# Two order strings rewritten, and one stride moved from a transpose's output to another's PSUM input, in an fp32 attention-and-SwiGLU kernel

## The chip, the cores and the metric

The kernel runs on one core of one Trainium2 chip. The metric is the device time of one execution in microseconds, as the median of several runs. The profile comes from one further execution.

## The reference

Eight batches of 512 tokens and 32 states, eight heads of 64. Tokens read the states and states read the tokens by softmax attention; the result of both, 544 rows of 512 per batch, goes through an RMS norm and a SwiGLU network of width 1536.

```python
scores = x @ state^T / 8;   a  = softmax(scores)    # per batch and head: 512 x 32
xread  = a @ state
scores2 = state @ x^T / 8;  a2 = softmax(scores2)   # 32 x 512
sread  = a2 @ x
rows = concat([xread, sread]) as (4352, 512)        # heads side by side
xn  = rows / sqrt(mean(rows^2) + 1e-6) * rms_g
out = (silu(xn @ w_gate) * (xn @ w_val)) @ w_out
```

Activations are fp32. The three weights come as 64-bit floats, which the kernel turns into fp32 itself from their bits.

## The kernel before, in words

The work is a set of Python generators, one for each kind of step. A `yield` ends a step, and strings of letters (`ORDER`, `PERIOD`, `STATES`) say in which order the steps are taken. The instructions of PE (TensorE), DVE (VectorE), ACT (ScalarE), POOL (GpSimd) and SP (the queue of most DMAs) stand in each engine's queue in just that order, so the strings are the schedule. Each engine works its queue in order and waits at the head of it.

**Batch 0 and the start (`ORDER`).** 18 weight pieces arrive as raw 64-bit words. Letter `e` is ScalarE's part of the conversion (L222, L224, L227), `d` VectorE's (L248, L251, L255, L260), four instructions of 128 by 1024 for a piece. Converted gate and value weights go out to a scratch tensor and are fetched again for each later batch. `a` and `A` are `tokens_read` of batches 0 and 1: load and transpose the tokens on TensorE (L306, copied by ScalarE at L308), scores (L333), transposes of scores (L342), softmax, and the read-out (L426), squares, and the norm: L353, POOL's power (L277), L284 along rows, and L439, which scales the attention weights. `s` and `S` are `states_read`. `v` multiplies a weight pair by the states (L554, copied at L566), so that `h`, `t`, `u` are hidden products with the attention weights (L597), their silu (L603) and gate (L607). `p` and `c` project (L803) and copy out. `k` sums output weights (L846). `z` is `keep_awake`, a matmul on the identity whose result nobody reads (L1135).

**Batches 1 to 7 (`PERIOD`).** The string is walked once per batch. Hidden products use seven products in place of eight (`hidden_seven`: L701 on TensorE, L747 to L754 on ScalarE, L763, L776 to L788 on VectorE), the projection seven times seven in place of 64 (`project_twice`: L1003; its inner sums are L1051 to L1057, its outer ones L1062, its additions L1043, its last combinations on POOL L1029 to L1034, stores at L1111). While batch b is multiplied, the tokens and states of batch b+1 are read (`a`, `s`). For batches 2 to 7, the transposes of the tokens don't run on TensorE: VectorE transposes 32 by 32 blocks (L316), a DMA writes them to scratch (L318, on ScalarE's queue) and four read them back across partitions (L323). Each token tensor is loaded so that four consecutive tokens lie in one partition, which leaves the columns of the scores in an order that has to be put right somewhere. Letters `q` and `G` (sums of weight quarters, and the first fetches of them) have steps in batch 1 alone; a letter with no stream is skipped.

In the last period no batch follows. There the letter `a` takes steps of `state_norm` (L519, L524, L528, the power, L284, then L534 and L686 in one step) and of the sums of the first weight piece for the states (L658 to L664), but through `paced`, which lets eleven calls pass and then takes one step in three calls.

**The states (`STATES`).** At last all 256 state rows go through the network by L701 and L866.

Of the kernel before, what the change touches and what calls it, by code (L numbers as in the profile page):

```python
# [8 lines left out]
F32 = mybir.dt.float32  # L9
# [4 lines left out]
ACTF = mybir.ActivationFunctionType  # L14
# [3 lines left out]
P = 128  # L18
# [1 line left out]
W_BUFS = 3  # L20

ORDER = (
    "aaaaaadaaaaadeeaaeaaeadaaaeeaaaeaaadaadeaaeadddzzzzzzzzzzzzzzzzzzzzzzzzaaadaddee"
    "daaaeazzzzzzzzzzzvvzaddeadvazzzAeeadeaedzzzhtdddAehAuAhdAeAeeAAtdpdddedpddvvvhue"
    "hddeeAehddteeppdudhdededApdvpddsdtshusevevhAeedehtApdAdeAAeupeedhdAdtApddhAvAsev"
    "uvsdApdhAetdsdhphAepeAsedAtesddeesuddpAddshdudApevdvpsAvAsheeedAdthheudAedtpeAdd"
    "dAApeddAApehuvvvApedhSShtAhAdduSdhASStSpASSAASukkkSpAkwSSsswwSwpwckcSkkpkkkpckck"
    "wwww"
)

PERIOD = (
    "vfhththahhtalhhuxxuttqqhufxtvqhhhtahahuuqquuutqhaquhaqttahhhhxthhuxquutxhuhuttuv"
    "kkqxxxvxhaqqhhGthhqqauuuxxqqqhkaatuGhqkuuthuaattaaahuqaqhuhuthtsusushhhuutthhGug"
    "huuqqpqtpaauufhuagpkuppkkpqsaakfgkkappcpkpakkcqkpkppapppppcqqkkkkpakppppppkppkpp"
    "pcaaaaaksssaaqaaakpppckkpppksappkskkagggcksakaakppppaooaoposkppppgkkkpasakoawssw"
    "xosspxfxlccoowxxxf"
)
# [8 lines left out]
def kernel(  # L46
# [32 lines left out]
    SCALE = 1.0 / D ** 0.5  # L79
# [3 lines left out]
    one = ctx.enter_context(tc.tile_pool(name="one", bufs=1))  # L83
# [206 lines left out]
    def scores(b, packed, soft):  # L290

        xb = x_sb[b]
        stT = one.tile([P, 4, Ns], F32, name="stT")
        tp = aps.tile([P, 4, Ns], F32, name="at")
        TE.transpose(out=tp.rearrange("p j n -> p (j n)"),
                     in_=packed.rearrange("p e d -> p (e d)"), identity=ident)
        yield
        VE.tensor_copy(stT, tp)
        yield "step"

        if b < 2:
            xT = one.tile([P, 4, NC, P], F32, name="xT", tag="xT")
            for c in range(NC):
                tp = aps.tile([P, 4, P], F32, name="at")
                for j in range(4):
                    TE.transpose(out=tp[:, j, :], in_=xb[:, c, P * j:P * j + P], identity=ident)  # L306
                yield
                SE.copy(xT[:, :, c, :], tp)  # L308
                yield "step"
            xT = xT.rearrange("p j c t -> p j (c t)")  # L310
        else:


            xB = one.tile([P, 4, 4, Ns, NC], F32, name="xB", tag="xT")
            for q in range(4):
                VE.transpose(out=xB[:, q].rearrange("p j t c -> p j c t"), in_=xb[:, q // 2::2, :, Ns * (q % 2):Ns * (q % 2) + Ns])  # L316
                yield
            nc.scalar.dma_start(out=x_d[b % 2].rearrange("q g f r -> (g f) q r"),  # L318
                                in_=xB.rearrange("p q j t c -> p q (j t c)"))
            yield  # L320
            xT = one.tile([P, 4, 4, P], F32, name="xG", tag="xT")
            for q in range(4):
                nc.scalar.dma_start(  # L323
                    out=xT[Ns * q:Ns * q + Ns].rearrange("f g j r -> f g (j r)"),
                    in_=x_d[b % 2][q].rearrange("g f r -> f g r"))
                yield
            xT = xT.rearrange("p g j r -> p j g r")


        sp = [aps.tile([P, S], F32, name="at") for e in range(2)]  # L330
        for j in range(4):
            for e in range(2):
                TE.matmul(out=sp[e][Ns * j:Ns * j + Ns, :], lhsT=stT[D * e:D * e + D, j, :],  # L333
                          rhs=xT[D * e:D * e + D, j],
                          start=True, stop=True)
        yield


        sS = read[b] = (one if b else x_0).tile([P, 2, NC, P], F32, name="sS")
        eS = one.tile([P, 2, S // Ns, Ns], F32, name="eS", tag="eS")  # L340
        for e in range(2):
            VE.transpose(out=eS[:, e].rearrange("p k n -> p (k n)"), in_=sp[e])  # L342
# [100 lines left out]
    def states_read(b):  # L443

        xb, sS = x_sb.pop(b), read.pop(b)
        e2 = one.tile([P, 4, 2, NC, Ns], F32, name="e2")
# [8 lines left out]
        VE.tensor_scalar(s2, m2, -SCALE, None, op0=ALU.mult)  # L455
        yield
        for e in range(2):
            to = exps[:, e] if b < 2 else e2[:, :, e].rearrange("p g c t -> p g t c")
            SE.activation(out=to, in_=(sS[:, e] if b < 2 else
                                       sS[:, e].rearrange("p g (t c) -> p g t c", c=NC)), func=ACTF.Exp, scale=SCALE,  # L460
                          bias=s2[:, e:e + 1], accum_out=z2[:, e:e + 1])
            yield "step" if e else None

# [685 lines left out]
        for part in own:  # L1149
            yield from part[0]  # L1150

    def paced(steps):

        yield from range(11)
        while True:
            if next(steps, done) is done:
                break
            yield from range(3)
        while True:
            yield  # L1160

    parts_0, banks_0 = {}, []
    load_state(0)
    load_x(0, nc.scalar, nc.sync)
# [15 lines left out]
    with tc.manual_schedule(**by_hand):  # L1180
# [7 lines left out]
        for b in range(1, B):  # L1188
            h, t, u = hidden_seven(S, weights_of(b), lambda b=b: tokens_of(b), True)
            p, c, k, o = project_twice(b, store_tokens(b))  # L1190
            own = [own_weights(b, mp) for mp in range(2, NM // 2)]
            then = [own_weights(b + 1, mp) for mp in range(2)] if b + 1 < B else []
            others = None
# [55 lines left out]
```

## Time and profile before

| | |
|---|---|
| median of 3 runs | 773.39 us (773.28 to 774.97) |
| the profiled execution | 772.66 us |
| its span | 770.5 us |
| PE busy in the span | 750.9 us (97%) |
| DVE busy | 618.1 us (80%) |
| ACT busy | 354.4 us (46%) |
| POOL busy | 296.2 us (38%) |
| first hidden product of batch 0 (L597) | 36.11 us |
| first hidden product of batch 1 (L701) | 137.72 us |
| one period, batches 2 to 6 | 81.7 to 81.9 us |

The span is what the profiler saw on the core; the execution's own time is 2.16 us longer. A line of a group gives the code line, the engine, output from input by the program's names, how often, the busy time and the mean duration of one, and the idle time of the engine just ahead of it with what ended it. In a timeline, the bracket at the end of a line is such an idle time. An fp32 matmul is shown as two records.

### The profile page before, as it was taken

The page shows a single profiled execution, that of the slowest core. Times are in us where ns is not written, and L with a number is a line of the kernel's source. Part 1 is how long each engine was busy: PE and PEld are TensorE (multiplying, and loading weights), DVE is VectorE, ACT ScalarE, POOL GpSimd, SP SyncE. Part 2 cuts the span into 40 slices and gives each one's busy share as a digit, 9 for nine tenths or more (in the row PEclk, how much of TensorE's full clock was granted, in tenths as well). Part 3 has the DMA queues.
Part 4 walks back from the last instruction along what each step waited for, and adds up shares of the span by engine and source line. Part 5 has one row for each costly group of instructions (what it writes and reads, how often), then busy time and mean ns, then how long its engine had stood idle before and what let it go on. Part 6 is the DMA issues. An engine that isn't in the chain of part 4 may idle for free.

```text
span 770.5 us, 14346 instructions
## 1 busy us (share of the span) xinstructions
PE 750.9 (97%) x5608; PEld 594.9 (77%) x5608; DVE 618.1 (80%) x1000; ACT 354.4 (46%) x548; POOL 296.2 (38%) x379
## 2 busy tenths in 40 slices
PE   6999999999999999999999999999999999999998
PEld 5643445778877898879977997889878988899996
DVE  4999988679957997689957995799579974799561
ACT  5798875454235523554165424552355236511220
POOL 2100003884585225642375039402852256324400
PEclk9999999999999999999999999999999999999999
DMA  9877844855786266825684367616862665052311
GB/s 292 252 255 245 312 179 130 320 173 199 255 260 236 55 231 224 310 58 198 188 306 130 127 202 256 237 43 234 255 236 53 233 199 223 1 200 75 124 55 27
DMA packets 61890, 146.15 MB, mean 190 GB/s; under 512 B 15744, under 2 KB 32640, under 8 KB 54912
## 3 DMA queue, kind: packets, MB, share of 16 engines
q1 hardware_dynamic: 48704, 125.78, 47.7%
q10 hardware_dynamic: 13120, 19.47, 8.8%
q8 instruction: 44, 0.72, 0.4%
q14 instruction: 22, 0.18, 0.1%
HBM read 116.46 MB, written 28.77 MB: 188 GB/s over the span
## 4 chain that ended last, share of the span: by engine, by line
PE 67%; DVE 27%; issue 3%; ACT 1%; POOL 1%; DMA 0%; SPq 0%; DVEq 0%; POOLq 0%
PE f L701 31%; PE f L1003 12%; PE f L803 5%; PE pv L597 5%; DVE hb L1062 4%; PE at L554 3%; PE pv L554 3%; DVE hb L776 3%; PE f L866 2%; DVE h L1057 2%; DVE h L1051 2%; DVE h L1053 2%; DVE g L763 1%; DVE hs L782 1%; DVE kept L1043 1%
## 5 line engine op out<-in xcount | busy, mean ns | idle before, releaser
L701 PE MATMUL f<-aT_s,v 128*128 128x256 f32 x504 | 117.7, 381 | 0.0
L701 PEld LDWEIGHTS f<-aT_s,v 128*128 128x128 f32 x504 | 94.7, 190 | 19.2 <-ACT v L566 5.9
L763 DVE TENSOR_TENSOR g<-g,f 128x512 f32<-128x512 f32 (+1 forms) x96 | 61.2, 648 | 51.1 <-PE f L701 31.0
L1029 POOL TENSOR_TENSOR kept<-kept 128x256 f32<-128x256 f32 x28 | 23.4, 838 | 202.8 <-DVE z L414 113.3
L701 PE MATMUL f<-aT_t,vs 128*128 128x256 f32 x336 | 87.5, 384 | 0.5 <-DVE g L763 0.4
L1003 PE MATMUL f<-w,h 128*128 128x128 f32 x588 | 75.4, 278 | 4.3 <-DVE h L1053 4.3
L754 ACT ACTIVATE hb<-g 128x1024 f32<-128x1024 f32 (+1 forms) x48 | 48.2, 1005 | 67.6 <-DVE g L763 67.6
L701 PEld LDWEIGHTS f<-aT_t,vs 128*128 128x128 f32 x336 | 62.2, 190 | 18.1 <-issue 6.9
L1003 PEld LDWEIGHTS f<-w,h 128*128 128x128 f32 x588 | 69.8, 192 | 6.7 <-DVE h L1053 5.8
L1013 ACT COPY kept<-f 128x512 f32<-128x512 f32 (+1 forms) x56 | 28.8, 540 | 73.2 <-PE f L1003 68.9
L566 ACT COPY v<-pv 128x512 f32<-128x512 f32 x42 | 22.6, 592 | 79.5 <-PE pv L554 78.1
L277 POOL TENSOR_TENSOR ri<-ss,mhalf 128x4 f32<-128x4 f32 x8 | 11.3, 1407 | 118.8 <-DVE ss L357 116.2
L581 POOL TENSOR_TENSOR vs<-v 128x256 f32<-128x256 f32 x42 | 31.3, 744 | 61.7 <-ACT v L566 61.7
L701 PE MATMUL f<-aT_t,v 128*128 128x256 f32 x168 | 44.4, 387 | 1.6 <-DVE c L763 1.5
L803 PE MATMUL f<-wo,hb 128*128 128x512 f32 x96 | 44.7, 598 | 0.0
L752 ACT COPY g<-f 128x512 f32<-128x512 f32 (+1 forms) x48 | 26.9, 561 | 38.1 <-PE f L701 38.1
L597 PE MATMUL pv<-aT_s,v 128*128 128x512 f32 x96 | 44.2, 597 | 0.0
L701 PE MATMUL f<-aT_s,vs 128*128 128x256 f32 x168 | 43.8, 383 | 0.0
L776 DVE TENSOR_TENSOR hb<-hb,c 128x512 f32<-128x512 f32 (+1 forms) x48 | 39.2, 816 | 5.0 <-ACT hb L754 4.8
L1003 PE MATMUL f<-wo,h 128*128 128x128 f32 x336 | 42.3, 275 | 0.0
L1003 PE MATMUL f<-wo,hb 128*128 128x128 f32 x336 | 42.1, 275 | 0.0
L1003 PEld LDWEIGHTS f<-wo,hb 128*128 128x128 f32 x336 | 40.3, 192 | 0.4
(179 smaller groups left out, 1704.9 us busy)
## 6 DMA issues: line engine op xcount, KB each, us to landing
w_m<-w_d SPq DMA_DIRECT2D x48, 1024.0 KB, 6.6
w<-t_d SPq DMA_DIRECT2D x49, 576.0 KB, 4.1
out_dram<-kept SPq DMA_DIRECT2D x56, 128.0 KB, 3.4
raw<-in_moe_w_val_dram SPq DMA_DIRECT2D x6, 1024.0 KB, 5.2
raw<-in_moe_w_out_dram SPq DMA_DIRECT2D x6, 1024.0 KB, 7.5
w_d<-w_m SPq DMA_DIRECT2D x6, 1024.0 KB, 4.9
x_b<-in_x_dram SPq DMA_DIRECT2D x6, 1024.0 KB, 7.6
x_d<-xB ACTq DMA_DIRECT2D x6, 1024.0 KB, 4.2
```

The costliest lines, as they stand in the source:

```text
L554: TE.matmul(out=pv[e][Ns * j:Ns * j + Ns, :], lhsT=stT_g[b][D * e:D * e + D, j, :], rhs=w[D * e:D * e + D, j].rearrange("p m k f -> p (m k ...
L581: GE.tensor_tensor(out=vs[:, 0], in0=a21, in1=a22, op=ALU.add)
L597: TE.matmul(out=to[0], lhsT=lhs(i, k), rhs=r, start=(i == 0), stop=(i == len(rhs) - 1))
L701: TE.matmul(out=ps[:, i, 0:half], lhsT=l[:, i, :], rhs=r, start=(start and i == 0 and k == 0), stop=(k == len(lhs) - 1), skip_group_check= ...
L752: SE.copy(gates(q)[1], q["x"][:, :, 0:half])
L754: SE.activation(out=hb[:, 2 * mp:2 * mp + 2, 0:n].rearrange("p m (c t) -> p m c t", c=2), in_=q["g"][:, :, :, 0:half], func=ACTF.Silu if s ...
L763: VE.tensor_tensor(out=to, in0=to, in1=q[ps][:, :, 0:half], op=ALU.add)
L776: VE.tensor_tensor(out=part, in0=part, in1=val, op=ALU.mult)
L803: TE.matmul(out=banks[r], lhsT=hb[:, m, P * r:P * r + P], rhs=wo[:, m, :], start=(m == 0), stop=(m == NM - 1))
L1003: TE.matmul(out=to[half][:, slot, :], lhsT=lhs[:, k, :], rhs=rhs[:, k, :], start=(fresh and n in (0, 4) and k == 0), stop=(k == QM - 1), s ...
L1013: SE.copy(k[:, 4 * i:4 * i + 4 - i], banks[name][i])
L1062: VE.tensor_tensor(out=to[:, k:k + QM], in0=a[:, k:k + QM], in1=b[:, k:k + QM], op=ALU.subtract)
```

## The change

Three things change.

1. **Layout.** For batches 2 to 7, the transposed blocks `xB` keep the order in which VectorE produces them (c, then t) where they were written with c innermost. The columns of the scores are then in another order, and the transposes of the scores (L342 before) read PSUM with t outside c, so that the attention weights of the tokens end in the order as before. The copy of the scores for the states and the exponential (L459 before) then read and write contiguous runs.
2. **The first order string.** `ORDER` is replaced by another of the same length with the same number of each letter. It begins with ten `z`, and has 26 `z` after batch 0's scores.
3. **The period string.** It is split into three: `FIRST` for batch 1, which is the old string; `PERIOD` for batches 2 to 6, which is the old string without `q` and `G`; and `LAST` for batch 7, in which only letters with steps are left and the nine steps of `a` have places of their own. `paced` goes. The first two `a` of `LAST` are where their steps were taken before; the other seven come later.

```diff
 ORDER = (
-    "aaaaaadaaaaadeeaaeaaeadaaaeeaaaeaaadaadeaaeadddzzzzzzzzzzzzzzzzzzzzzzzzaaadaddee"
-    "daaaeazzzzzzzzzzzvvzaddeadvazzzAeeadeaedzzzhtdddAehAuAhdAeAeeAAtdpdddedpddvvvhue"
...
+    "zzzzzzzzzzazadaaaaaaaaazzzdzzzzzzeaeeaaaaadaadeeaaaaeeezdeazdzzzzzzadeeeaadaadzz"
+    "zzzzzzzaaaaaddadzzzzvvvaaedzaAAdaaassdAAAAaAAeeAaAhtddddehehhuppedddddvtduppeeee"
...
+LAST = (
+    "vfhththhhthhuxxutthufxtvhhhthhuuuuuthuhtthhhhxthhuxuutxhuhuttuvkkxxxvxhhhthhuuux"
+    "xhktuhkuuthuattahuhuhuthtuuhhhuutthhughuuptpuufhuagpkuppkkpkfgkkppcpkpakkckpkppp"
+    "ppppckkkkpkppppppkppkpppcakaakpppckkpppkppkkkgggckkakppppooopokppppgkkkpakoopcco"
+    "o"
+)
...
-            xB = one.tile([P, 4, 4, Ns, NC], F32, name="xB", tag="xT")
+            xB = one.tile([P, 4, 4, NC, Ns], F32, name="xB", tag="xT")
             for q in range(4):
-                VE.transpose(out=xB[:, q].rearrange("p j t c -> p j c t"), in_=xb[:, q // 2::2, :, Ns * (q % 2):Ns * (q % 2) + Ns])
+                VE.transpose(out=xB[:, q], in_=xb[:, q // 2::2, :, Ns * (q % 2):Ns * (q % 2) + Ns])
...
-            VE.transpose(out=eS[:, e].rearrange("p k n -> p (k n)"), in_=sp[e])
+            VE.transpose(out=eS[:, e].rearrange("p k n -> p (k n)"),
+                         in_=(sp[e] if b < 2 else
+                              sp[e].rearrange("p (g c t) -> p g t c", g=4, c=NC)))
...
-            to = exps[:, e] if b < 2 else e2[:, :, e].rearrange("p g c t -> p g t c")
-            SE.activation(out=to, in_=(sS[:, e] if b < 2 else
-                                       sS[:, e].rearrange("p g (t c) -> p g t c", c=NC)), func=ACTF.Exp, scale=SCALE,
+            to = exps[:, e] if b < 2 else e2[:, :, e].rearrange("p g c t -> p g (c t)")
+            SE.activation(out=to, in_=sS[:, e], func=ACTF.Exp, scale=SCALE,
                           bias=s2[:, e:e + 1], accum_out=z2[:, e:e + 1])
...
-                others = paced(step for part in (state_norm(), sums_of_w([0])) for step in part)
-                streams["a"] = others
-            for stream in PERIOD:
-                if stream in streams:
-                    step = next(streams[stream], done)
-                    assert step is not done or b + 1 == B
-            assert all(next(stream, done) is done for stream in streams.values() if stream is not others)
+                streams["a"] = (step for part in (state_norm(), sums_of_w([0])) for step in part)
+            for stream in FIRST if b == 1 else LAST if b + 1 == B else PERIOD:
+                next(streams[stream])
+            assert all(next(stream, done) is done for stream in streams.values())
```

More of the change, by code (lines that the diff above doesn't have):

```diff
@@ L22 @@
 ORDER = (
-    "aaaaaadaaaaadeeaaeaaeadaaaeeaaaeaaadaadeaaeadddzzzzzzzzzzzzzzzzzzzzzzzzaaadaddee"
-    "daaaeazzzzzzzzzzzvvzaddeadvazzzAeeadeaedzzzhtdddAehAuAhdAeAeeAAtdpdddedpddvvvhue"
-    "hddeeAehddteeppdudhdededApdvpddsdtshusevevhAeedehtApdAdeAAeupeedhdAdtApddhAvAsev"
-    "uvsdApdhAetdsdhphAepeAsedAtesddeesuddpAddshdudApevdvpsAvAsheeedAdthheudAedtpeAdd"
-    "dAApeddAApehuvvvApedhSShtAhAdduSdhASStSpASSAASukkkSpAkwSSsswwSwpwckcSkkpkkkpckck"
+    "zzzzzzzzzzazadaaaaaaaaazzzdzzzzzzeaeeaaaaadaadeeaaaaeeezdeazdzzzzzzadeeeaadaadzz"
+    "zzzzzzzaaaaaddadzzzzvvvaaedzaAAdaaassdAAAAaAAeeAaAhtddddehehhuppedddddvtduppeeee"
+    "ddvvdddeeeedAAddhhtuhhpeAddeApAtddeesvuvddveApdddhheedtupddeeehtAAAddhueeeddsApA"
+    "AAdpepvvevAsddddedddphtsssseeehuhAdtssddpdshuedeedpvvvAeApdeAehtdhhAueddppAdddtA"
+    "eeddpAheuSSAAAeAAvAvvpehhtSSddhdAAASSpAtuSShSSSdkAuwwsSSSpcpcskpwckkkkkkkkpwkkwc"
     "wwww"
@@ L31 @@
 PERIOD = (
+    "vfhththahhtalhhuxxutthufxtvhhhtahahuuuuuthauhattahhhhxthhuxuutxhuhuttuvkkxxxvxha"
+    "hhthhauuuxxhkaatuhkuuthuaattaaahuahuhuthtsusushhhuutthhughuuptpaauufhuagpkuppkkp"
+    "saakfgkkappcpkpakkckpkppapppppckkkkpakppppppkppkpppcaaaaaksssaaaaakpppckkpppksap"
+    "pkskkagggcksakaakppppaooaoposkppppgkkkpasakoawsswxosspxfxlccoowxxxf"
+)
+FIRST = (
     "vfhththahhtalhhuxxuttqqhufxtvqhhhtahahuuqquuutqhaquhaqttahhhhxthhuxquutxhuhuttuv"
@@ L36 @@
     "xosspxfxlccoowxxxf"
+)
+LAST = (
[3 more added lines that the diff above has]
+    "o"
 )
@@ L311, in scores @@
         else:
-            xB = one.tile([P, 4, 4, Ns, NC], F32, name="xB", tag="xT")
+            xB = one.tile([P, 4, 4, NC, Ns], F32, name="xB", tag="xT")
             for q in range(4):
-                VE.transpose(out=xB[:, q].rearrange("p j t c -> p j c t"), in_=xb[:, q // 2::2, :, Ns * (q % 2):Ns * (q % 2) + Ns])
+                VE.transpose(out=xB[:, q], in_=xb[:, q // 2::2, :, Ns * (q % 2):Ns * (q % 2) + Ns])
                 yield
             nc.scalar.dma_start(out=x_d[b % 2].rearrange("q g f r -> (g f) q r"),
-                                in_=xB.rearrange("p q j t c -> p q (j t c)"))
+                                in_=xB.rearrange("p q j c t -> p q (j c t)"))
             yield
@@ L1150, in first_products @@
             yield from part[0]
[L1152 to L1160, printed above, removed]
     parts_0, banks_0 = {}, []
@@ L1192 @@
             then = [own_weights(b + 1, mp) for mp in range(2)] if b + 1 < B else []
-            others = None
             streams = {"h": h, "t": t, "u": u, "p": p, "c": c, "k": k,
```

## The prediction, made before the changed kernel was run

> **What bounds the kernel now.** I read the busy times per stage first, then the TensorE and VectorE timelines of one steady batch period, the rows by form, and the two ends of the kernel. All line numbers are those of the kernel before.
>
> The busy times in stretches (us, then PE, PEld, DVE, ACT, POOL busy with counts, clock, DMA share, GB/s), for batch 0 from its first hidden product, batch 3's period and the last period:
>
> ```profile
> 35.95:137.72 101.77, 101.75 (x527) 44.23 (x526) 95.52 (x124) 78.42 (x100) 9.05 (x9) 1.00 0.66 230
> 305.70:387.40 81.70, 81.16 (x671) 68.06 (x678) 66.86 (x115) 35.65 (x59) 35.23 (x46) 1.00 0.59 194
> 633.00:712.86 79.86, 78.70 (x578) 69.50 (x577) 61.37 (x93) 29.82 (x49) 36.33 (x46) 1.00 0.35 123
> ```
>
> TensorE leaves 0.02 us idle in batch 0, 0.54 us in a steady period of 81.7 us, and 1.16 us in the last. A steady period can therefore gain at most 0.54 us from anything that VectorE or ScalarE does faster. The 0.54 us are two waits in the TensorE timeline:
>
> ```profile
> 343.86 1.13 PE L701 MATMUL f<-aT_t,v 128*128 128x256 f32 x4 [0.15 <-DVE c L763]
> 365.97 1.60 PE L1003 MATMUL f<-w,h 128*128 128x128 f32 x12 [0.39 <-DVE h L1053]
> ```
>
> Both are waits for VectorE. Its own timeline of that period:
>
> ```profile
> 314.22 2.12 DVE L316 STREAM_TRANSPOSE xB<-x_b 128x512 f32<-128x512 f32 x2 [0.22 <-DMA x_b<-in_x_dram]
> ...
> 325.41 1.29 DVE L763 TENSOR_TENSOR g<-g,f 128x512 f32<-128x512 f32 x2 [1.04 <-ACT g L752]
> ...
> 333.07 1.48 DVE L763 TENSOR_TENSOR g<-g,f 128x512 f32<-128x512 f32 x2 [2.00 <-PE f L701]
> ...
> 340.14 1.30 DVE L342 STREAM_TRANSPOSE eS<-at 128x512 f32<-128x512 f32 x2
> ```
>
> From 333.07 to past 366 VectorE has no gap; that stretch sets the two waits. Before it VectorE waits for TensorE (2.00 us). The reader should see that the four xB transposes (314 to 324) lie ahead of that wait, and the two eS transposes (340) inside the gapless stretch.
>
> [...](busy us, mean ns, idle before):
>
> ```profile
> L316 DVE STREAM_TRANSPOSE xB<-x_b 128x512 f32<-128x512 f32 x24 | 26.6, 1150 | 1.4 <-DMA x_b<-in_x_dram 1.4
> ...
> L419 DVE STREAM_TRANSPOSE aT_s<-eS 128x512 f32<-128x512 f32 x16 | 11.3, 705 | 0.2
> ...
> L342 DVE STREAM_TRANSPOSE eS<-at 128x512 f32<-128x512 f32 x16 | 10.5, 689 | 1.1 <-PE at L333 1.1
> ```
>
> Writing with 16 bytes between neighbours (L316) takes 1150 ns, contiguous 705 ns. [...]
>
> ```profile
> 6.01 0.44 PE L295 MATMUL at<-ident,rows 128*128 128x128 f32 x1 [6.01 <-DMA rows<-in_state_dram]
> 6.24 3.31 PE L306 MATMUL at<-ident,x_b 128*128 128x128 f32 x16
> 10.26 1.09 PE L333 MATMUL at<-xT,stT 64*32 64x512 f32 x16 [0.71 <-ACT xT L308]
> 11.28 10.63 PE L1135 MATMUL f<-ident 128*128 128x256 f32 x48
> ```
>
> Sixteen transposes take 3.31 us, 0.20 us apart; eight later ones take 1.04 us at 41.80, 0.10 us apart. [...]L1057 takes 0.55 us alone and 1.08 us at 337.34, under L584 on POOL.
>
> **The change part by part, against the profiled execution's 772.66 us** (span 770.5 and 2.16 around it; it lies 0.73 below the median of 773.39, which I add to the deltas).
>
> Layout, six periods (batches 2 to 7 are read in the periods of 1 to 6). Four xB transposes go from 1.15 to about 0.705 us: 1.8 us less VectorE work. Two exponentials of L459 read and write contiguously: their median is 1.20 us for the strided batches and 0.705 us at the least, 1.0 us less ScalarE. The two eS transposes now read PSUM with 128 bytes between neighbours. The savings fall where VectorE then waits 2.00 us for TensorE, and where ScalarE's exponentials (351.6 and 364.0) have no waiter: nothing. The DMA that stores xB (L318, on ScalarE's queue) goes up to 1.8 us earlier, but its readers (L323) stand behind copies of v that wait for TensorE until 330: nothing. If that cover were gone, the ceiling is still 0.54 x 6 = 3.2 us. The cost of the strided PSUM read is not in the trace for this size. Bounds: 0 ([...]689 ns) and 0.445 us each (the rate of L316); it cannot gain, since no work is removed there. I take 0, because the half-rate price is shown only for SBUF writes; both ends go into the range. Taken: 0 for six periods.
>
> The first order string. Ten warming matmuls (L1135, two records each) go ahead of the first transpose; all four transposes of batch 1's tokens (L306) go ahead of the first hidden product (L597, 36.11); some exponents and VectorE steps are permuted. SP's order is unchanged.
> - The warming ones can start at 1.40, when POOL has finished ident. Warm they are 10.63/48 = 0.22 us per record, cold twice that. [...]they end near 7.4, where the first transpose now starts at 6.01, 1.4 later. Then the 16 transposes run warm behind ScalarE's four copies at about 0.55 us: L333 follows the first transpose by 3.5 us (0.22, one more warming matmul 0.43, 0.44 and 0.2, 4 x 0.55) instead of 4.25. So L333, and with it the gapless VectorE chain from L342 (11.44) to L439 (36.06), start 0.7 later. Bounds: -0.8 (no cold cost; then VectorE is held by the raw piece until 10.6) and +3.2 (all twenty records cold).
> - In VectorE's chain to L439 only one copy (L298, 0.2) is added; the two maxima (L452) fall into the wait for POOL's power and L284. +0.2.
> - The fourth token transpose now needs the PSUM buffer that L439 still reads, so it runs after L439 and ahead of the first L597: +0.45.
> - TensorE's batch 0 (no idle time) loses the 16 transposes: 0.44 + 0.88 + 0.44 = 1.76 us. VectorE, 95.52 of 101.77 busy, must keep up: adding up its steps, the second weight pair is finished at 46.3 where TensorE asks at 46.4, and later gaps are 0.5 us at most, which replace like ones now. -1.76.
> Sum: 0.7 + 0.2 + 0.45 - 1.76 = -0.4.
>
> The last period. The state norm's VectorE block (L534, L686: 683.65 to 686.9, 3.2 us) moves behind the inner sums of the fourth outer product, the sums of the first weight piece (L658 to L664) go later, the last of them between the two halves of the final add (L1043).
>
> ```profile
> 683.65 1.65 DVE L534 SCALAR_TENSOR_TENSOR xsT<-xsT,rms_g,at 128x256 f32<-128x256 f32 x4
> ...
> 705.46 1.15 DVE L1043 TENSOR_TENSOR kept<-kept,f 128x512 f32<-128x512 f32 x2
> ```
>
> ```profile
> 693.69 1.60 PE L1003 MATMUL f<-w,h 128*128 128x128 f32 x12 [0.79 <-DVE h L1053]
> ...
> 712.86 1.16 PE L701 MATMUL f<-x_t,v 128*128 128x128 f32 x8 [0.36 <-ACT g L747]
> ```
>
> The 0.79 us wait goes. But the wait at 712.86 is late next: ScalarE's L747 needs a buffer whose contents POOL combines (L1029 to L1034, 706.26 to 710.12) and SP then stores, landing 1.8 us after issue. Putting L664 (0.7 us, 1.1 while POOL reads) between the halves holds POOL's second step from 707.07 to about 707.7. The stores, L747 and TensorE come 0.6 us later than 712.86, with TensorE waiting for all of what it had gained. Bounds: -0.4 (the halves are early enough) and +1.0. Taken: +0.6. The period string of the middle batches orders the same steps as before.
>
> Total -0.4 + 0 + 0.6 = +0.2: **773.6 us**.
>
> **Rivals.**
> - Strided PSUM reads run at half rate. Place: the gapless stretch at 340. Price 12 x 0.445 = 5.3 us, all of it passed on, since TensorE already waits for VectorE there: 778.9, slower. It decides from 0.11 us per transpose on (1.35/12). For it: L316's price[...].
> - The cheaper transposes count after all, by taking away the two waits: at most 3.2 us, with the rest as forecast 770.4. For: VectorE is 99% busy from 334 to 366. Against: the 2.00 us wait ahead of that stretch.
> - The start is warm in time[...]: -0.8 in place of +0.7, no hold of 0.45, and the last period keeps 0.4: 770.2 to 771.5, say 770.8. For: the first transposes are indeed at half pace now. Against: twenty records ahead of data that arrive at 6.0.
> - The warming matmuls stay cold: +3.2 in place of 0.7, 776.1.
>
> **How the numbers follow.** A difference under 0.2%, 1.55 us, is about what a measurement of this kernel cannot tell from none. Forecast, within 0.2%: 0.35, own range 771.9 to 774.9. Half-rate reads 0.26 and cold start 0.06, slower: 0.32. Cheaper transposes counting 0.10 and warm start 0.23, faster: 0.33. The range runs from the warm case to the half-rate case, 770.3 to 779.0.
>
> **What would show it.** The eS transpose at 0.69 us and the waits of 0.15 and 0.39 us unchanged: layout is free. At 1.14 us: they sum to 1.4 us per period. First transpose at 7.4, first hidden product at 37.4, first L701 about 137.3: start as worked out. No wait near 693 and some 2 us of wait at the first state product: last period as worked out. A period shorter than 81.2 us, or an earlier first hidden product, would prove me wrong.

## The result and the profile after

| | before | after |
|---|---|---|
| median, first five runs of each on one chip | 773.82 us (773.28 to 774.97) | 770.49 us (770.43 to 771.45) |
| ratio | | 0.9965 [0.9954, 0.9976] |
| the profiled execution | 772.66 us | 770.64 us |
| its span | 770.5 us | 768.9 us |
| DVE busy / ACT busy | 618.1 / 354.4 us | 608.3 / 350.5 us |
| first hidden product of batch 0 | 36.11 us | 35.47 us |
| first quarter product of batch 1 | 137.72 us | 135.96 us |
| second product of the states | 712.86 us | 711.19 us |

The changed kernel is 0.35% faster, below the point forecast of 773.6 and at the lower end of its range (770.3). In 22 later runs its median was 771.28 against 773.29 (35 runs): 9 of them, all with a mean TensorE clock of 0.995 or 0.996, took 773.4 to 774.6 us, and the other 13 have a median of 770.83.

In the changed kernel the numbers of the lines are 12 to 14 higher. The busy times in stretches, as shown of before (stretch, its length, then PE, PEld, DVE, ACT, POOL busy, clock, DMA share, GB/s), for batch 0 from its first hidden product, batch 3's period, the last period:

```profile
35.47:135.96 100.49, 100.16 (x511) 42.35 (x510) 92.47 (x121) 79.68 (x100) 6.15 (x8) 1.00 0.68 240
303.91:385.59 81.68, 81.29 (x663) 68.33 (x662) 66.14 (x115) 34.94 (x59) 34.87 (x45) 1.00 0.59 194
631.16:711.19 80.03, 78.51 (x577) 69.49 (x577) 61.01 (x93) 29.89 (x49) 36.89 (x46) 1.00 0.35 123
```

From its first hidden product, batch 0 is 1.12 us shorter (before, 101.61 us from 36.11; the stretch in the prediction begins 0.16 us ahead of that product) and it starts 0.64 us earlier. The steady period is what it was (81.70 before). The TensorE timeline of that period and of the last one has these two waits:

```profile
364.24 1.60 PE L1016 MATMUL f<-w,h 128*128 128x128 f32 x12 [0.39 <-DVE h L1066]
...
711.19 1.16 PE L714 MATMUL f<-x_t,v 128*128 128x128 f32 x8 [1.52 <-ACT g L760]
```

The wait of 0.39 us is unchanged and the one of 0.15 us, which only this period of before has, is gone, without the period becoming shorter. The 0.79 us at 693 are gone, and 1.52 in place of 0.36 us stand ahead of the second product of the states. VectorE's groups by form (busy us, mean ns, idle before):

```profile
L328 DVE STREAM_TRANSPOSE xB<-x_b 128x512 f32<-128x512 f32 x24 | 16.2, 696 | 0.8 <-DMA x_b<-in_x_dram 0.8
...
L354 DVE STREAM_TRANSPOSE eS<-at 128x512 f32<-128x512 f32 x16 | 10.6, 691 | 1.4 <-PE at L345 1.4
```

The transposes that wrote with a stride went from 1150 to 696 ns; the 16 that read PSUM, 12 of them now with a stride, take 691 ns on average and 717 at most (689 on average before). The start, in TensorE's timeline of after:

```profile
7.34 0.27 PE L307 MATMUL at<-ident,rows 128*128 128x128 f32 x1
...
9.16 1.14 PE L318 MATMUL at<-ident,x_b 128*128 128x128 f32 x8 [0.24 <-ACT xT L320]
10.98 1.09 PE L345 MATMUL at<-xT,stT 64*32 64x512 f32 x16 [0.68 <-ACT xT L320]
```

The first transpose is at 7.34 us and the scores at 10.98, as forecast (+0.7). What follows is not as forecast. All engines of before around the norm of batch 0:

```profile
31.93 0.15 DVE L357 TENSOR_SCALAR ss<-at 128x4 f32<-128x4 f32 x1
32.00 1.21 DVE L255 SCALAR_TENSOR_TENSOR ex<-raw,ex 128x1024 int32<-128x1024 int32 x1
32.16 1.93 POOL L277 TENSOR_TENSOR ri<-ss,mhalf 128x4 f32<-128x4 f32 x1 [26.64 <-DVE ss L357]
...
34.84 1.22 DVE L439 TENSOR_TENSOR aT_s<-aT_s,at 128x1024 f32<-128x1024 f32 x1 [0.36 <-PE at L284]
```

and of after:

```profile
31.81 0.16 DVE L371 TENSOR_SCALAR ss<-at 128x4 f32<-128x4 f32 x1
31.88 1.27 DVE L466 TENSOR_REDUCE m<-sS 128x1 f32<-128x512 f32 x2
32.04 1.02 POOL L289 TENSOR_TENSOR ri<-ss,mhalf 128x4 f32<-128x4 f32 x1 [26.50 <-DVE ss L371]
...
34.20 1.22 DVE L453 TENSOR_TENSOR aT_s<-aT_s,at 128x1024 f32<-128x1024 f32 x1
...
34.88 0.66 PE L318 MATMUL at<-ident,x_b 128*128 128x128 f32 x4 [0.68 <-ACT xT L320]
35.47 3.70 PE L610 MATMUL pv<-aT_s,v 128*128 128x512 f32 x8
```

POOL's power takes 1.02 in place of 1.93 us, and the fourth token transpose (34.88) waits for ScalarE's copy and not for L453: it starts while L453 still runs (to 35.42).

### The profile page after: what moved, and what is told of

It is laid out like the page before. It is cut to its first block, busy times and chain, and to the rows that moved or that the text cites. A ratio compares the mean times of both kernels' runs of the same rounds, so it can differ in the third digit from the quotient of the medians.

```text
span 768.9 us, 14347 instructions
## 1 busy us (share of the span) xinstructions
PE 752.1 (98%) x5608; PEld 595.0 (77%) x5608; DVE 608.3 (79%) x1000; ACT 350.5 (46%) x548; POOL 292.0 (38%) x379
## 4 chain that ended last, share of the span: by engine, by line
PE 62%; DVE 27%; POOL 4%; issue 3%; ACT 2%; DMA 1%; SPq 0%; DVEq 0%; ACTq 0%; POOLq 0%
PE f L714 26%; PE f L1016 14%; PE f L816 6%; PE pv L610 5%; DVE hb L789 3%; DVE hb L1075 3%; PE at L567 3%; PE f L879 2%; DVE h L1070 2%; PE pv L567 2%; DVE g L776 2%; DVE h L1064 2%; DVE hs L795 2%; DVE h L1066 2%; DVE kept L1056 1%
## 5 line engine op out<-in xcount | busy, mean ns | idle before, releaser
L1042 POOL TENSOR_TENSOR kept<-kept 128x256 f32<-128x256 f32 x28 | 23.5, 839 | 199.7 <-DVE z L428 113.1
L289 POOL TENSOR_TENSOR ri<-ss,mhalf 128x4 f32<-128x4 f32 x8 | 10.4, 1295 | 116.3 <-DVE ss L371 113.8
L789 DVE TENSOR_TENSOR hb<-hb,f 128x512 f32<-128x512 f32 (+1 forms) x48 | 31.2, 650 | 15.9 <-PE f L714 15.4
```

The lines of the kernel that those rows point to most:

```text
L789: VE.tensor_tensor(out=part, in0=part, in1=val, op=ALU.mult)
L1042: GE.tensor_tensor(out=k[:, 1:3], in0=k[:, 0:1].to_broadcast([P, 2, QD]), in1=k[:, 1:3], op=ALU.add)
```

## The experiments

The theory after the result: the gain is in the first order string alone, in two places, VectorE's chain from the scores to the first hidden product and the 16 transposes that leave batch 0. Rivals: the layout counts; the last period counts; the leading warming matmuls are the gain. Most edits are to `ORDER` and are shown as the first piece of the string that changes (`...` where it goes on; letters that change places further on are not shown). What the traces say of the parts, in us (each column is a difference of two start times in one trace; eS is the first transpose of the scores, L342 of before; the power's input is L357):

| kernel | start of eS | eS to L357 | L357 to first hidden product | that to first quarter product |
|---|---|---|---|---|
| before | 11.44 | 20.49 | 4.18 | 101.61 |
| layout_only | 12.51 | 20.46 | 4.19 | 101.60 |
| last_only | 12.85 | 20.47 | 4.19 | 101.61 |
| six_before | 10.88 | 20.48 | 4.19 | 101.61 |
| after | 12.16 | 19.65 | 3.66 | 100.49 |
| after_again | 12.55 | 19.63 | 3.66 | 100.51 |
| fill | 11.28 | 19.64 | 3.66 | 100.52 |
| fill_again | 11.92 | 19.65 | 3.66 | 100.52 |
| ten_fill | 12.93 | 19.63 | 3.66 | 100.51 |
| zero_fill | 12.76 | 19.65 | 3.65 | 100.50 |
| sum_later | 10.76 | 19.63 | 3.66 | 100.49 |
| power_exposed | 10.77 | 19.64 | 4.48 | 100.59 |
| norm_cover | 11.66 | 20.51 | 3.66 | 103.18 |
| vector_mixed | 11.70 | 21.31 | 4.20 | 101.61 |
| tokens_moved | 12.57 | 22.33 | 6.15 | 100.55 |
| tokens_moved2 | 12.53 | 20.53 | 6.87 | 100.87 |
| order_only | 13.66 | 19.64 | 4.74 | 101.59 |
| warm_first | 12.49 | 20.99 | 4.22 | 101.60 |

Only the first column differs between kernels of the same order; the others repeat to 0.03 us.

### Which of the three parts

**layout_only**: the three edits to `xB`, `eS` and the exponentials, in the kernel before.

> The kernel before with the layout part alone (xB kept contiguous, the scores' transposes reading PSUM with t outside c, the exponentials contiguous); both order strings as before. Theory (the gain is the first order string alone): within 0.3 us of the kernel before; the TensorE waits of 0.15 us at the first quarter products and 0.39 us at the outer product are unchanged in the steady periods, which stay at 81.7 to 81.9 us. Rival (the 1.8 us of VectorE work and 1.0 us of ScalarE work saved per period count): 1 to 3 us faster, periods shorter by up to 0.5 us each.

773.03 us against 773.06, ratio 0.9999 [0.9991, 1.0007]. From its TensorE timeline and its groups by form:

```profile
367.17 1.60 PE L1004 MATMUL f<-w,h 128*128 128x128 f32 x12 [0.39 <-DVE h L1054]
```

```profile
L316 DVE STREAM_TRANSPOSE xB<-x_b 128x512 f32<-128x512 f32 x24 | 16.2, 695 | 1.8 <-DMA x_b<-in_x_dram 1.7
```

10.4 us of transposes less on VectorE (26.6 to 16.2) are worth nothing. The theory had the 0.15 us wait staying; it went, for no gain.

**order_only**: `ORDER` of the changed kernel, in the kernel before.

> The kernel before with the first order string of the changed kernel and nothing else. Theory (the whole gain is here): 2.0 to 3.3 us faster than before, first hidden product near 35.5 us and first quarter product near 136.0 us in the trace, everything later shifted by the same amount. Rival (layout or last period carry a part): less than 1.5 us faster.

771.41 us against 773.06, ratio 0.9992 [0.9980, 1.0003]: 1.65 us less by the medians, where the theory had 2.0 to 3.3, and an interval that takes in no change. Of 14 runs ten lie at 770.66 to 771.84, below every one of the 48 runs of before (771.95 and more), and four at 774.46 to 774.71, the four with a mean clock of 0.995; that widens the interval. The profiled run was one of the four. Its stretches (clock third from the end):

```profile
33.00:34.00 1.00, 1.00 (x10) 0.81 (x9) 1.00 (x4) 0.40 (x2) 0.46 (x1) 1.00 0.77 213
34.00:35.00 1.00, 0.56 (x5) 0.39 (x4) 1.00 (x3) 0.79 (x2) 0.56 (x1) 0.89 1.02 418
35.00:38.00 3.00, 2.33 (x11) 1.93 (x10) 3.00 (x4) 1.51 (x2) 0.00 (x0) 0.50 0.43 175
38.00:41.00 3.00, 3.00 (x6) 1.37 (x5) 2.96 (x4) 2.95 (x4) 0.00 (x0) 0.50 0.49 153
41.00:42.00 1.00, 1.00 (x3) 0.30 (x2) 0.04 (x1) 0.39 (x2) 0.00 (x0) 0.69 1.04 406
42.00:43.00 1.00, 1.00 (x4) 0.52 (x3) 0.00 (x0) 1.00 (x2) 0.00 (x0) 1.00 0.48 184
```

From 35 to 41 us the granted clock is 0.50. If the stretches at 0.89 and 0.69 are made up of 0.5 and 1.0 alone, they have 0.22 and 0.62 us of it: an estimate of 6.84 us at half clock, from 34.78 to 41.62. The first hidden product (38.04 us in this trace) and what follows lie in that stretch, so its places don't test the theory; from eS to L357, ahead of it, the trace has the 19.64 us of the changed kernel. So the gain is in this string, as the ten runs and the two other parts together show, but the string has a risk of its own, which none of the theories had.

**last_only**: `FIRST`, `PERIOD` and `LAST` in place of `PERIOD` and `paced`, in the kernel before.

> The kernel before with the split of the period string alone. Theory: the 0.79 us wait near 693 us goes and the wait at the second state product grows by as much, so 0.0 to 0.2 us from the time before. The prediction's own step: 0.6 us slower. Rival (the 0.79 us are kept): 0.4 to 0.8 us faster.

773.30 us against 773.06, ratio 1.0001 [0.9994, 1.0007], with a wait of 1.51 us ahead of the second product of the states. As the theory says; 0.6 us slower is outside the interval (1.0007 is +0.5).

### The leading warming matmuls and the half clock

**warm_first**: the first ten `z` of the kernel before moved to the front.

```diff
-    "aaaaaadaaaaadeea...aadeaaeadddzzzzzzzzzzzzzzzzzzzzzzzzaaad...
+    "zzzzzzzzzzaaaaaadaaaaadeea...aadeaaeadddzzzzzzzzzzzzzzaaad...
```

> The kernel before with its first ten warming matmuls moved from the row of 24 to the very start, ahead of the first transpose; nothing else moves. The prediction's step: they end near 7.4 us, VectorE's chain starts 0.7 us later and so does the first hidden product: 0.7 us slower. Rival one (the warm start is the gain): 1 us or more faster. Rival two (they only take away a run-to-run part that lies in the cold start): the trace shows +0.7 us, but the spread of the times falls from about 1.7 us to under 1 us and the median is at or below that of the kernel before.

774.85 us, ratio 1.0026 [1.0016, 1.0035]: slower, by more than any of the three said, and for another reason. The row of 24 that lost ten had filled the time until VectorE's weights; TensorE now waits 1.84 and 1.61 us there, and the trace shows a granted clock of 0.91 from 22 to 23 us, 0.50 from 23 to 26 and 0.89 from 26 to 27, some 3.4 us at half clock by the same estimate as in order_only. The experiment doesn't isolate the start.

**after_again**: the changed kernel.

> The changed kernel once more, beside the kernel before on the same chip, for its spread: the kernel with the first order string alone had most of its times at 770.7 to 771.8 us and some at 774.5 to 774.7 us, the latter with a mean granted clock of 0.995. Theory (the order string leaves too little TensorE work between 30 and 36 us[...]): the changed kernel has the same two groups, in about a quarter of its runs, and a median 1.5 to 2.5 us below before. Rival (the layout or the last period guard against it): all runs near 770.5 us, 3 us below before.

771.28 us against 773.29, ratio 0.9985 [0.9975, 0.9995]: both groups, 9 of 22 over 773.3 us, all 9 with a mean clock of 0.995 or 0.996, more than the quarter that the theory had. No trace was taken of one of the 9; that they are at half clock where order_only was is inferred from their mean clock.

**fill** and **fill_again** (one and the same kernel, on two occasions): four of the ten leading `z` moved into TensorE's gaps.

```diff
-    "zzzzzzzzzzaza...zzzzvvvaaedzaAAdaaassdAAAAaAAeeAaAh
+    "zzzzzzaza...zzzzzvvvaaedzaAzAdaaassdAAAzAaAzAeeAaAh
```

> The changed kernel with four of the ten leading warming matmuls moved: one each behind the row ahead of the first product of the states, behind the transpose of batch 1's states, behind the second and behind the third of batch 1's token transposes (27 to 35 us), where TensorE waits. Theory ([...]the leading row ends past 7.4 us in many): no run with a clock under 0.998 and none over 773 us, median 0 to 1.5 us below the changed kernel. Rival (the two groups come from somewhere else): the same two groups as the changed kernel.

> The fill kernel once more, six leading warming matmuls and four in the gaps. Theory: 769.3 to 770.5 us median, 2.8 to 3.8 us under the kernel before, no run over 772 us. Rival (its low times were chance, and one run at a clock of 0.997 in a sister kernel was the start of the second group): a median at the changed kernel's 771.3 us with runs over 773 us.

770.06 us (768.68 to 770.93), ratio 0.9956 [0.9944, 0.9968], and 769.70 us (768.49 to 770.53), ratio 0.9953 [0.9940, 0.9965]: 3.2 and 3.6 us under before, no run over 771 us. This version beats both kernels.

**ten_fill** (the four added, all ten kept in front), **zero_fill** (the four, none in front), **six_before** (the kernel before with six `z` put in front) change the number of leading ones alone.

> The changed kernel with its ten leading warming matmuls, and four more added in TensorE's gaps between 27 and 35 us. Theory[...]: no run over 772.5 us, median 770.5 to 771.0 us. Rival[...]: the group at 773.4 to 774.6 us stays.

> The fill kernel without any of its six leading warming matmuls. Theory (without them the transposes and in most runs the scores of batch 0 run at half clock): the first of VectorE's scores transposes starts at 11.4 to 12.9 us in place of 10.8 to 11.3, and the kernel is 0.6 to 1.7 us slower than with six. The prediction's own view (leading matmuls only delay the first transposes): 0 to 0.7 us faster than with six.

> The kernel before with six warming matmuls added ahead of its first transpose, nothing else. Theory: they end by 6.6 us, the scores of batch 0 then never run at half clock and the scores' transposes on VectorE start near 11 us in place of 11.4 to 12.9: 0.8 to 1.6 us faster than before, with a smaller spread. The prediction's view: up to 0.5 us later, 0.3 us slower.

The theory of ten_fill put the second group down to too little TensorE work between 30 and 36 us, its rival to the ten leading ones. ten_fill: 771.36 us, ratio 0.9975 [0.9964, 0.9985], 770.66 to 772.20: with filled gaps no run of 8 has a mean clock under 0.999, though the median is above the 771.0 of the theory. zero_fill: 771.19 us, ratio 0.9973 [0.9962, 0.9985]. six_before: 771.91 us against 773.29, ratio 0.9987 [0.9980, 0.9993] (some 1.0 us by the ratio, 1.4 by the medians); its runs spread over 2.4 us, where before's spread over 2.7, so the smaller spread of the theory is not shown. So six in front are worth 1.0 to 1.5 us over none, in either kernel, and in the changed one 1.3 to 1.7 over ten; with five to eight runs each, the intervals of fill and fill_again just touch those of zero_fill and ten_fill, and six_before with 21 is the firmest. The scores' products of layout_only, whose start is that of before,

```profile
6.08 3.71 PE L306 MATMUL at<-ident,x_b 128*128 128x128 f32 x16
10.46 1.96 PE L333 MATMUL at<-xT,stT 64*32 64x512 f32 x16 [0.68 <-ACT xT L308]
```

and of six_before:

```profile
6.95 1.96 PE L306 MATMUL at<-ident,x_b 128*128 128x128 f32 x12 [0.17 <-DMA x_b<-in_x_dram]
9.59 1.09 PE L333 MATMUL at<-xT,stT 64*32 64x512 f32 x16 [0.68 <-ACT xT L308]
```

Without leading work the scores take 1.96 us in four of seven traces with before's start, and 1.09 in the other three, the profiled run of before among them. "Half clock" in these expectations is a reading of such paces: the granted clock is shown as 1.00 from 6 to 12 us in before and in layout_only alike. With six the first transpose is at 5.9 to 6.7 us (five traces), with ten at 7.3 to 8.8 (five traces).

### The parts of the order string

**norm_cover**: the two maxima under the power.

```diff
-    ...vvzaddeadvazzzAeeadeaedzzzh
+    ...vvzaddeassvazzzAeeadeadedzzzh
```

> The kernel before with the two maxima of the states' scores (L452) taken right after the norm's sum (L357), and VectorE's conversion steps L255 and L260 of that piece one place later: POOL's power then runs under instructions with one SBUF input. Theory (part of the early first hidden product comes from the power no longer contending): power 1.02 in place of 1.94 us, first hidden product 0.6 to 0.9 us earlier than 36.1, end 0.4 to 0.9 us faster. Rival (batch 0 is bound by VectorE's sum of work, so the place of two steps does not matter): the power is faster but the first quarter product stays at 137.7 us, within 0.2 us of before.

773.81 us, ratio 1.0010 [1.0001, 1.0018]: slower. The power took 1.02 us and the way to the first hidden product is 0.52 us shorter; batch 0 then took 1.57 longer. All engines of that kernel:

```profile
39.33 1.28 ACT L603 ACT_TABLE_LOAD   x1
...
40.62 0.60 ACT L603 ACTIVATE t<-pv 128x512 f32<-128x512 f32 x1
...
41.27 1.98 PE L597 MATMUL pv<-aT_s,v 128*128 128x512 f32 x4 [1.31 <-ACT t L603]
```

ScalarE's conversions went late with VectorE's, its silu behind them, and TensorE waits 1.31 us. The theory has the mechanism and not the time. The first quarter product, which the rival left at 137.7 us, came at 139.0.

**power_exposed**: the reverse, in the fill kernel.

```diff
-    ...aAzAdaaassdAAAzAaAzAee...
+    ...aAzAdaaadssAAAzAaAzAee...
```

> The changed kernel with four leading warming matmuls moved into TensorE's gaps (the fill kernel), and in it the conversion step with two SBUF inputs (L255 in the numbering of before) put back right behind the norm's sum, ahead of the two maxima. Theory (the power contends with it): power 1.94 in place of 1.02 us, from the norm's sum to the end of the scaling of the weights 4.1 to 4.5 in place of 3.6 us, first hidden product 0.5 to 0.9 us later, batch 0 unchanged from there (100.5 us), so 0.5 to 0.9 us slower than the fill kernel. Rival (the wait moves to the conversion, nothing is lost): within 0.2 us of the fill kernel, 3 us under before.

```profile
30.48 1.21 DVE L267 SCALAR_TENSOR_TENSOR ex<-raw,ex 128x1024 int32<-128x1024 int32 x1
30.64 1.94 POOL L289 TENSOR_TENSOR ri<-ss,mhalf 128x4 f32<-128x4 f32 x1 [25.11 <-DVE ss L371]
...
33.32 1.22 DVE L453 TENSOR_TENSOR aT_s<-aT_s,at 128x1024 f32<-128x1024 f32 x1 [0.44 <-PE at L296]
...
34.40 0.66 PE L318 MATMUL at<-ident,x_b 128*128 128x128 f32 x4 [0.24 <-ACT xT L320]
34.89 3.60 PE L610 MATMUL pv<-aT_s,v 128*128 128x512 f32 x8
```

In the trace the theory holds: power 1.94 us, and the first hidden product 0.82 us later from L357 (4.48 for 3.66). The time, 769.84 us, ratio 0.9962 [0.9950, 0.9975], doesn't show it: five runs that spread over 2 us don't resolve 0.8, with starts that differ by as much. The power takes 1.94 us beside the step with two SBUF inputs (L267) and, in after, 1.02 beside the reductions (L466), which have one.

**vector_mixed**: VectorE's order up to L357 as in the changed kernel (but for the copy L298), the other engines as before.

```diff
-    "aaaaaadaaaaadeeaaeaaeadaaaeeaaaeaaadaadeaaeadddzzzzzzzzzzzzzzzzzzzzzzzzaaadaddee"
-    "daaaeazzzzzzzzzzzvvzaddeadvazzz...
+    "aaddaaaaaaaaaeeaaeaaeaadaeeadaaeeezzzzzzzzzzzzzzzzzzzzzzzzaadadadaadaadadddaaaae"
+    "eaezzzzzzzzzzzvvzaadadaeadvazzz...
```

> The kernel before with VectorE's order between the scores' transposes (L342) and the norm's sum (L357) taken from the changed kernel: the same instructions, the conversion steps put between the softmax steps that need each other's result. All other engines keep their order. Theory (a VectorE instruction that needs the result of the one just ahead starts about 0.1 us later than one that does not): from the first of L342 to L357 19.6 us in place of 20.5, first hidden product 0.8 us earlier relative to the scores, end 0.8 us faster. Rival (the chain is shorter in the changed kernel because of what ScalarE and TensorE do): L342 to L357 stays at 20.4 to 20.5 us and the time within 0.3 us of before.

774.16 us, ratio 1.0010 [1.0001, 1.0018]: slower, and from eS to L357 21.31 us, more than the theory's 19.6 and the rival's 20.5. VectorE's timeline:

```profile
27.48 0.68 DVE L436 TENSOR_TENSOR sq<-sq 128x512 f32<-128x512 f32 x1
29.67 0.69 DVE L436 TENSOR_TENSOR sq<-sq 128x512 f32<-128x512 f32 x1 [1.50 <-ACT sq L433]
```

VectorE came to its first L436 15.78 us after eS, where before needs 16.70 (28.14 less 11.44) for the same instructions: 0.92 us less. But the last transpose of the weights now stands behind a conversion step, so the read-out starts later, and the squares stand between conversions in ScalarE's queue: 1.50 us of wait take it back. The 0.92 us are seen at single instructions. In before a multiplication ahead of a step that doesn't read its result, and the transpose behind that step; then the same multiplication ahead of the transpose that reads it:

```profile
17.37 0.69 DVE L417 TENSOR_TENSOR eS<-eS,z 128x512 f32<-128x512 f32 x1
17.98 0.68 DVE L260 SCALAR_TENSOR_TENSOR w_m<-raw,ex 128x512 f32<-128x512 f32 x1
18.59 0.70 DVE L419 STREAM_TRANSPOSE aT_s<-eS 128x512 f32<-128x512 f32 x1
...
20.62 0.69 DVE L417 TENSOR_TENSOR eS<-eS,z 128x512 f32<-128x512 f32 x1
21.35 0.71 DVE L419 STREAM_TRANSPOSE aT_s<-eS 128x512 f32<-128x512 f32 x1
```

0.61 us to the next start where it doesn't need the result, 0.73 where it does; it isn't the transpose that is late, since behind L260 it too starts after 0.61. So the pair that needs the result costs 0.12 us more.

**tokens_moved** and **tokens_moved2**: batch 1's transposes ahead of the first hidden product of the kernel before, in two placements.

```diff
-    ...azzzzzzzzzzzvvzaddeadvazzzAeeadeaedzzzh
+    ...aAAzzzzzzzzzzzvvzaddeadvaAAAAzzzeeaAAdeAaAedzzzh
```

```diff
+    ...azzzzzzzzzzzvvzaddeadvazAAAAAAaAAeeAadeAedzzzzzh
```

> The kernel before with the transposes of batch 1's states and tokens (L295, L306, their copies L298 and L308) ahead of the first hidden product, in the places of the changed kernel; the warming matmuls and all else as before. The prediction's terms: +0.2 for the copy, +0.45 for the fourth transpose that is held, -1.76 for the 16 transposes: 1.1 us faster. Theory: the fourth transpose is not held, the copy is hidden, and batch 0 shortens by 1.1 to 1.8 us: 1.1 to 1.8 us faster. Rival (ScalarE's four copies only displace conversion steps, and VectorE is late by as much): under 0.5 us.

> The kernel before with batch 1's transposes ahead of the first hidden product once more, but behind the first two products of the states and behind the norm's sum, so that they hold up neither; VectorE's last conversion step of that piece goes behind L439. Theory: from the norm's sum to the end of L439 at most 0.2 us more than before's 4.13, batch 0 from the first hidden product to the first quarter product 100.5 in place of 101.6 us, end 0.9 to 1.1 us faster. The prediction's terms: 0.65 us later at the first hidden product, batch 0 shorter by 1.76. Rival (where they stand, ScalarE's copies delay the conversion and VectorE gives it back): batch 0 not under 101.2 us.

776.56 us, ratio 1.0043 [1.0031, 1.0055], and 775.55, ratio 1.0030 [1.0022, 1.0039]: both slower, because both placements hold up the way to the first hidden product, the first by a buffer that a square frees late (1.78 us) and by one that L439 still reads, the second by the warming matmuls that I left behind the last transpose (2.3 us). The fourth transpose of tokens_moved:

```profile
39.26 0.66 PE L306 MATMUL at<-ident,x_b 128*128 128x128 f32 x4 [0.88 <-DVE aT_s L439]
```

There the fourth transpose stands behind L439 in the order, and the hold that the prediction expected is real. In tokens_moved2, as in the changed kernel, it stands ahead of L439 and waits 0.68 us for ScalarE's copy instead. Batch 0 from the first hidden product shows what was asked: 100.55 and 100.87 us, so 1.06 and 0.74 us shorter, not 1.76. The times test nothing else.

### The last period

**sum_later**: in the fill kernel, the last sum (L664 of before, L677 here) behind the second half of the final add.

```diff
-    ...pokppppgkkkpakoopccoo
+    ...pokppppgkkkpkoopaccoo
```

> The fill kernel with the last of the sums of the first weight piece for the states (L664 in the numbering of before) behind both halves of the final add instead of between them. The prediction's step (L664 there holds POOL's second combination and with it the stores, ScalarE's copy and TensorE by 0.6 us): the wait at the second product of the states falls from 1.5 to about 0.9 us and the kernel is 0.6 us faster than fill. Theory (POOL's second round starts only when ScalarE has copied the last product, at the same moment as before): wait 1.4 to 1.6 us, within 0.2 us of fill.

771.25 us, ratio 0.9966 [0.9953, 0.9980]; five runs between 768.91 and 771.70, whose interval overlaps that of fill. Three of them, at 771.25 to 771.70, have a mean clock of 0.997 or 0.998, though the start is that of fill. The profiled run of warm_first, with some 3.4 us at half clock, has 0.997, so by their mean clock these three had about as much, half of order_only's 6.84: the filled gaps do not exclude it. No trace of such a run was taken. The wait grew from 1.51 to 1.98 us. POOL:

```profile
702.37 1.23 POOL L1042 TENSOR_TENSOR kept<-kept 128x256 f32<-128x256 f32 x1 [1.90 <-issue]
...
706.69 1.17 POOL L1042 TENSOR_TENSOR kept<-kept 128x256 f32<-128x256 f32 x1
707.94 1.05 POOL L1044 TENSOR_TENSOR kept<-kept 128x256 f32<-128x256 f32 x1
```

and in the fill kernel:

```profile
703.25 0.77 POOL L1042 TENSOR_TENSOR kept<-kept 128x256 f32<-128x256 f32 x1 [1.90 <-issue]
...
707.12 1.17 POOL L1042 TENSOR_TENSOR kept<-kept 128x256 f32<-128x256 f32 x1
```

The last product before the states starts 1.83 us after POOL's first L1042 in both (704.20, 705.08): L677 did not hold POOL. What moved is POOL's first step, 1.23 in place of 0.77 us, with v's sums, which have two SBUF inputs, now due beside it by the order; that they are the cause is inferred. ScalarE had copied the last product at 706.22, and POOL's second round begins only at 706.69, as its own first round ends (706.73). The prediction's step expected a gain where there is none, and the theory, for which that copy starts the second round, missed the 0.47 us too.

## Why the prediction was wrong

| step | forecast | from the two traces |
|---|---|---|
| start, to the scores' transposes | +0.7 | +0.72 |
| from there to the first hidden product: copy +0.2, held transpose +0.45 | +0.65 | -1.36 |
| batch 0 without 16 transposes | -1.76 | -1.12 |
| layout, and the middle periods | 0 | -0.1 |
| last period | +0.6 | +0.2 |
| sum | +0.2 | -1.7 |

**The layout** was right, by its reason: the work saved lies ahead of a wait for TensorE, and the strided PSUM read costs nothing (691 ns on average for 689). The rival that the strided read pays L316's price (1150 for 705 ns, which it calls half rate) is refuted, and so is the rival that the cheaper transposes count. (The reading that VectorE has no gap from 333.07 us on misses two, of 0.11 us at 333.87 and 0.17 at 334.73; it changes nothing.)

**The failed step is the second:** forecast 0.65 us later, measured 1.36 earlier. The prediction took VectorE's chain as the old one plus a copy, and said of the permuted steps only that two maxima fall into the wait for POOL's power. It had read that L1057 takes 0.55 us alone and 1.08 under L584 on POOL, but did not look for the same in the power and the step that the maxima displace (L255, with two SBUF inputs, under the power until then), and so put the swap at nothing. Two things happened. With the maxima beside it in place of L255, the power takes 1.02 us and not 1.93, and the way from L357 to the first hidden product is shorter: 0.52 us by before against after (4.18 to 3.66), 0.52 in norm_cover, 0.82 the other way in power_exposed, where the fourth transpose is late too. And the permuted steps stand between instructions that need each other's result: 0.84 us less from eS to L357 although the copy is in it, the mechanism shown by vector_mixed, up to the squares (0.92). The third term, the hold by L439, does not occur in the changed kernel, whose order has that transpose ahead of L439 (in tokens_moved, which has it behind, it does): it waits 0.68 us for ScalarE and is through by 35.5. The two shares are read from traces: norm_cover and vector_mixed, with one of them each, were slower, and only the whole string shows the gain in the times.

**Batch 0** has the mechanism right and the size too large: 1.12 us for 1.76. The 16 transposes that left had taken what was forecast, 1.75 us from start to start in the trace of before. TensorE gave 0.63 of it back. 0.33 is a new wait for the silu, which on ScalarE stands behind a conversion step and the copy of the fourth transpose:

```profile
39.50 3.70 PE L610 MATMUL pv<-aT_s,v 128*128 128x512 f32 x8 [0.33 <-ACT t L616]
```

The other 0.3 us are spread over TensorE's products in their new order: from start to start the 96 hidden ones take 42.49 us, with that wait, for 41.91, and the 96 of the projection 42.59 for 42.39. Why is open.

**The last period**: 0.79 us of wait go and 1.16 come back at the states, as said, but the period is only 0.17 us longer. That L664 holds POOL was wrong: sum_later moved it and gained nothing. In after, POOL's second round starts at 708.42, when ScalarE has copied the last product (708.40) and POOL's own first round ends (708.46); these two fall together. In sum_later it is the first round that counts.

**From the trace to the median.** Chain and batch 0 make 2.48 us between before and after, and 2.4 to 2.5 in every pair of traces with these two orders there (fill and its kin for the second) and a mean clock of 0.999 or more; the start adds 0.72 only against the trace of before that was at hand, one in which the scores took 1.09 us and not 1.96. Against the middle of the seven traces with that start (12.51 us) after's 12.16 and 12.55 add nothing, so that the forecast of +0.7 came true was luck. 773.29 less 2.48 is 770.8, the median of the 13 later runs of after at a mean clock of 0.999 or more. The forecast that the ten end near 7.4 us rested on its author's estimate of how long the slow pace lasts, which the trace of before doesn't show, and took the earliest case: with ten in front the first transpose came at 7.3 to 8.8. The warm rival came nearest in its number, 770.8, by a reason that only in part is the one found: it was right that the transpose is not held, but ten leading matmuls gain nothing, and six do. That the first five runs of each differ by 3.3 us and the later ones by 2.0 fits the spread of the start and the share of runs at the lower mean clock; no run shows it directly.

## What to carry to other kernels

When a schedule is rewritten, cost each new neighbourhood: what runs on VectorE beside a POOL instruction on the critical path, and whether two adjacent VectorE instructions need each other, since here such pairs were worth 0.5 and 0.8 us. One engine's better order is worth nothing without the others': the same VectorE order, alone, was slower. A warming matmul earned its place here ahead of late data (six in front: 1.0 to 1.5 us) and in TensorE's gaps (no mean clock under 0.999 in ten_fill, 9 of 22 at 0.995 or 0.996 without); count those that end before the data arrive, and look at several runs, since with ten in front the first transpose came anywhere from 7.3 to 8.8 us.

## What the runs showed of the hardware that was not expected

- VectorE's 16 transposes of 128 by 512 out of PSUM took 691 ns on average (717 at most) with 12 of them reading at 128 bytes between neighbours, 689 with all contiguous; writing SBUF with 16 bytes between neighbours took 1150 ns for 696.
- A VectorE instruction of 128 by 512 that needs the result of the one ahead (L419 behind L417 in before) started 0.73 us after it, one that doesn't (L260 behind L417) 0.61.
- With the first order string of the changed kernel, TensorE's work between 30 and 36 us, among transposes and one-column products, has gaps of 0.2 to 0.7 us. 9 of 22 runs of after_again have a mean clock of 0.995 or 0.996, and the trace of order_only, in a run at 0.995, has a granted clock of 0.50 for an estimated 6.84 us. With four more warming matmuls in TensorE's gaps between 27 and 35 us no run of 29 (fill, fill_again, ten_fill, zero_fill, power_exposed) has a mean clock under 0.999; three of five in sum_later have 0.997 or 0.998.
- POOL's power of 128 by 4 took 1.94 us beside a VectorE step with two SBUF inputs (power_exposed), 1.02 beside reductions (after).
